# Attention into a SwiGLU feed-forward on one core: a held product, an earlier Sqrt table, a transposed weight row, and half of each swap issued by GpSimd

## Chip, cores, metric

The kernel runs on 1 core of a Trainium2 chip. The metric is the device time in microseconds (us) of one execution, lower is better. Medians of several fast executions are quoted. The span of a profile is about 1.8 us shorter than the time of the same execution. One execution of the kernel before took 559.56 us; it is counted as disturbed, and medians and ratios here leave it out.

TensorE is PE below, VectorE DVE, ScalarE ACT, GpSimd Pool, SyncE SP. PSUM is the memory in which PE leaves its results until DVE or ACT has read them.

## The reference

```python
# q, k, v: (8, 12, 448, 64) float32
scores = q @ k.transpose(0, 1, 3, 2) / sqrt(64)
attn   = maximum(scores, 0) ** 2 / 448
x      = (attn @ v)                    # -> (8 * 448, 768), heads side by side
rms    = sqrt(mean(x * x, -1) + 1e-6)
xn     = x / rms * rms_g
g, val = xn @ w_gate, xn @ w_val       # 768 -> 1536 each
out    = (silu(g) * val) @ w_out       # 1536 -> 768
```

## The kernel before

A block is one of the 8 batch entries (b). While PE runs the gate and value matmuls of block b, the scores and values of block b + 1 are woven in as side tasks; then come output tiles, during which the normalisation of block b + 1 is done. `fb` counts the 12 column blocks of 128 gate and value columns.

Gate and value matmuls are 64 rows deep. Gate uses one half of PE's rows and value the other at the same time, so x is needed in both halves: `xT`, and `xD`, in which the two partition halves have changed places. For blocks 2 to 7 that exchange is done by DMA on the normed x.

```python
def leave(b, js):                       # attention values out of PSUM, on ACT
    ...
    if b > 1:
        square()
    for i, j in enumerate(js):
        nc.scalar.mul(out=xTs[b][:, j, :], in_=psAV[:, i, :], mul=ga_sb[:, j : j + 1])
    if b < 2:
        square()

def swap(b, j0, j1, eng=None):
    for hf in (0, 1):
        (eng or nc.sync).dma_start(
            out=xDs[b][hf * HALF : (hf + 1) * HALF, j0:j1, :],
            in_=xTs[b][(1 - hf) * HALF : (2 - hf) * HALF, j0:j1, :])

def norm_stat(b, ...):                  # sum of squares by PE, then
    nc.scalar.activation(out=half[:], in_=psSS, func=ACT.Sqrt, ...)
    nc.scalar.activation(out=warm_act[:], in_=eps_col[:], func=ACT.Silu)   # loads the Silu table
    nc.vector.reciprocal(out=half[:], in_=half[:])
    ...                                 # spread over partitions, scale x, swap

def blocnpart(b, fb, r0, r1):           # a unit: 2 of 12 rounds in blocks 1 to 7
    if r0 == 0:
        gvs[b, fb] = [ps_m.tile(...) for nm in ("psG", "psV")]   # 4 buffers: two pairs
    rounds(b, fb, gvs[b, fb], r0, r1)
    if r1 < 2 * KT:
        return
    ...
    nc.scalar.activation(out=s[:], in_=psG, func=ACT.Silu)
    nc.vector.tensor_tensor(out=hT[:, fb, o : o + S], in0=s[:], in1=psV, op=ALU.mult)

# weaving, NB = 72 units of gate and value
sides += along(0, (NB - 1) / len(steps), steps[:-3])        # attention of the next block
sides += [(NB - 1, steps[-3]), (NB - 0, steps[-2]), (NB, steps[-1])]
sides += [(NB + 2, norm_stat of b + 1), (NB + 2.1, norm_apply of b + 1)]   # cut to its sense
```

Of the kernel before, what the change touches and what calls it, by code (L numbers as in the profile page):

```python
# [8 lines left out]
FP32 = mybir.dt.float32  # L9
BF16 = mybir.dt.bfloat16  # L10
ALU = mybir.AluOpType
# [23 lines left out]
def kernel(  # L35
# [11 lines left out]
    nc = tc.nc  # L47
# [240 lines left out]
    def leave(b, js):  # L288

        psAV = psAVs.pop((b, js))  # L290
        last = (b, js[0]) == (0, HP - 1)

        def squares_of(i0, i1, o):
            nc.scalar.activation(out=o, in_=psAV[:, i0:i1, :], func=ACT.Square, scale=inv_attn)

        def square():
            if b < 2:
                squares_of(0, len(js), x2s[b][:, js[0] : js[-1] + 1, :])
                return
            t = sums[b]  # L300
            if js[0] == 0:
                squares_of(0, 2, t[:])
                return
            two = npool.tile([P, 2, S], FP32, name="x2f", tag="x2")
            for i in range(2):
                o = two[:, i, :]
                squares_of(i, i + 1, o)
                if js[0] == 2:
                    nc.vector.tensor_tensor(out=t[:, i, :], in0=t[:, i, :], in1=o, op=ALU.add)
                    if i:  # L310
                        nc.vector.tensor_tensor(
                            out=t[:, 0, :], in0=t[:, 0, :], in1=t[:, 1, :], op=ALU.add
                        )
                else:
                    nc.vector.tensor_tensor(out=t[:, 0, :], in0=t[:, 0, :], in1=o, op=ALU.add)

        if last:
            square()
            low, high, every = slice(0, HALF), slice(HALF, P), slice(0, P)
            j = js[0]  # L320
            for dst, to, fr in ((xTs, every, every), (xDs, low, high), (xDs, high, low)):
                nc.vector.tensor_scalar_mul(
                    out=dst[b][to, j, :], in0=psAV[fr, 0, :], scalar1=ga_sb[fr, j : j + 1]
# [5 lines that stand above are left out]
            nc.scalar.mul(out=xTs[b][:, j, :], in_=psAV[:, i, :], mul=ga_sb[:, j : j + 1])  # L329
        if b < 2:  # L330
            square()

    def cross(b, j, psAV):

# [1 line left out]
        for to, fr in ((low, high), (high, low)):  # L336
            nc.scalar.mul(out=xDs[b][to, j, :], in_=psAV[fr, 0, :], mul=ga_sb[fr, j : j + 1])

    def swap(b, j0, j1, eng=None):

        for hf in (0, 1):
            (eng or nc.sync).dma_start(
                out=xDs[b][hf * HALF : (hf + 1) * HALF, j0:j1, :],
                in_=xTs[b][(1 - hf) * HALF : (2 - hf) * HALF, j0:j1, :],
            )
# [166 lines left out]
    def rounds(b, fb, parts, r0, r1, x=None):  # L512

        for r in range(r0, r1):
            kt, own = r % KT, r < KT
            src = (x or (xTs[b], xDs[b]))[0 if own else 1]
            for part in range(2):
                prt = slice(part * HALF, (part + 1) * HALF)
                h = 2 * kt + (part if own else 1 - part)
                nc.tensor.matmul(  # L520
                    out=parts[part][:, :S],
                    lhsT=wgv_sb[prt, h, fb * P : (fb + 1) * P],
                    rhs=src[prt, kt, :],
                    start=(r == 0),
                    stop=(r == 2 * KT - 1),
                )
# [27 lines left out]
    def blocnpart(b, fb, r0, r1):  # L554
        if r0 == 0:
            gvs[b, fb] = [
                ps_m.tile([P, S], FP32, name=nm, tag="mm")[:] for nm in ("psG", "psV")
            ]
        rounds(b, fb, gvs[b, fb], r0, r1)
        if r1 < 2 * KT:  # L560
            return
        psG, psV = gvs.pop((b, fb))
        s = spool.tile([P, S], BF16, name="sil", tag="sil")
        nc.scalar.activation(out=s[:], in_=psG, func=ACT.Silu)  # L564
        hT, o = hidden(b)
        nc.vector.tensor_tensor(out=hT[:, fb, o : o + S], in0=s[:], in1=psV, op=ALU.mult)  # L566

    osts = {}

    def outproj(i, t, o, w):  # L570
# [59 lines left out]
    with fpool as fp:  # L630
        for nm, src, eng in (("k", k, nc.sync), ("q", q, nc.scalar)):
            first[nm] = fp.tile([PC, 2, NCH * D], FP32, name="first_" + nm, tag="first_" + nm)
            eng.dma_start(out=first[nm][:], in_=head_rows(src, 0, 0, 2))
        g_sb = wpool.tile([P, KT], FP32, name="g_sb", tag="rmsg")
        nc.sync.dma_start(out=g_sb[:], in_=moe_rms_g.rearrange("(kt p) -> p kt", p=P))
        load("k", 0, 2, 4)
        load("q", 0, 2, 4)
        ident = const.tile([PC, PC], BF16, name="ident", tag="ident")
        masks.make_identity(nc, ident[:])
        warm_in = const.tile([P, S], BF16, name="warm_in", tag="warm_in")  # L640
        nc.vector.memset(warm_in[:], 0.0)
        ones_bf = const.tile([P, P], BF16, name="ones_bf", tag="ones_bf")
        nc.vector.memset(ones_bf[:], 1.0)
        eps_col = const.tile([P, 1], FP32, name="eps_col", tag="eps_col")
        nc.vector.memset(eps_col[:], eps)
        warm_act = const.tile([P, 1], FP32, name="warm_act", tag="warm_act")
        nc.scalar.activation(out=warm_act[:], in_=eps_col[:], func=ACT.Sqrt)
        nc.vector.tensor_copy(out=ld["k", 0][:, :2, :], in_=first["k"][:])
        nc.scalar.copy(out=ld["q", 0][:, :2, :], in_=first["q"][:])
    ga_sb = wpool.tile([P, KT], FP32, name="ga_sb", tag="rmsga")  # L650
    nc.vector.tensor_scalar_mul(out=ga_sb[:], in0=g_sb[:], scalar1=inv_attn)
    load("k", 0, 4, 6)
    load("q", 0, 4, 6)
    load("v", 0, 0, 6)
    load("k", 0, 6, 12)
    load("q", 0, 6, 12)
    load("v", 0, 6, 12)

    def warm(n):

# [23 lines left out]
    with tc.tile_pool(name="qkT", bufs=2, side="right") as tp, tc.tile_pool(  # L684
        name="early", bufs=EB, side="right"
    ) as ep:
        late["qkT"], late["early"] = tp, ep
        warm(12)
        steps = attention_second(1)

        def early_block(fb):
            return [ps_m.tile([P, S], FP32, name="psE", tag="mm")[:] for _ in range(2)]

        units = attention_first(0)
        tail = len(units) - 4
        for n, fn in enumerate(units[:tail]):
            fn()
            if n % 3 == 2 and n < tail - 1:
                warm(2)


        raw_x = xTs[0], xDs[0]
        psSS = ps_m.tile([P, S], FP32, name="psSS", tag="mm")
        blocks = [early_block(0)]

        def part(fb, *rs):
            for r in rs:
                rounds(0, fb, blocks[fb], r, r + 1, raw_x)

        psAV4 = psAVs[0, (HP - 2,)]  # L710
        squares_last, leave_4, attend_5, leave_5 = units[tail:]
        squares_last()
        part(0, *range(HP - 2))
        pe_transposes(1, 0)
        leave_4()
        attend_5()
        leave_5()
        cross(0, HP - 2, psAV4)
        part(0, KT, HP - 2, KT + 1, KT + 2)
        norm_stat(0, psSS, steps.pop(0))  # L720
        norm_spread(0)
        blocks.append(early_block(1))
        part(1, *range(KT))
        part(0, HP - 1)
        part(1, *range(KT, KT + 3))
        part(0, KT + 4)
        steps.pop(0)()
        part(1, KT + 4)
        norm_apply(0)
        for fb in range(2):  # L730
            part(fb, KT + 3, KT + 5)
            early_out(0, fb, blocks[fb])
            if fb == 0:
                pe_transposes(1, 1)
        for fb in range(2, EB):
            blocks.append(early_block(fb))
            for r0 in range(0, 2 * KT, KT):
                steps.pop(0)()
                rounds(0, fb, blocks[fb], r0, r0 + KT, raw_x)
            early_out(0, fb, blocks[fb])  # L740
        main = gate_value(0, EB, KT // 2)
        sides = along(6.4, 2, [lambda fb=fb: early_scale(0, fb) for fb in range(EB)])
        sides += along(10.4, 2, [lambda fb=fb: early_rest(0, fb) for fb in range(EB)])
        sides += along(0, (len(main) - 1) / len(steps), steps[:-1])
        sides += [(26, lambda: trans_fill(2, 0))]
        alloc_ld(2)
        load("q", 2)
        load("k", 2)
        for s in range(4, FT // 2):
            fetch_o(s)  # L750
        sides += [(26, lambda: load("v", 2))]
        weave(main, sides)
# [55 lines left out]
```

## Time and profile before

| | before |
|---|---|
| median of fast executions | 443.1 to 443.5 us in the different sets of runs |
| span of the profile, first scores, end of PE | 441.23, 6.73, 437.19 us |
| PE from its first output matmul to its end | 363.20 us |

The prediction below shows the main lines. The step that a stall on the scores makes, in PE's timeline (start, length, engine, line, operation, output and inputs, shapes, count):

```profile
162.20 0.35 PE L520 MATMUL psV<-xD,wgv_sb 64*128 64x448 bf16 x1
162.62 0.36 PE L228 MATMUL psS<-qT,kT 64*128 64x448 bf16 x2
```

```profile
91.86 0.35 PE L520 MATMUL psG<-xT,wgv_sb 64*128 64x448 bf16 x1
92.05 0.35 PE L520 MATMUL psV<-xT,wgv_sb 64*128 64x448 bf16 x1
```

### The profile page before, as it was taken

Reading aid. Unit: us, or ns where it says so; the run is one execution under the profiler, and the core shown is the slowest. Engines: PE = TensorE matmul, PEld = TensorE weight load, DVE = VectorE, ACT = ScalarE, POOL = GpSimd, SP = SyncE. Lnnn points to the kernel's source line nnn. Section 1 sums busy time; section 2 is a strip of 40 time slices with the busy share of each in tenths; the row PEclk is TensorE's granted clock in tenths of the full one; section 3 lists DMA queues with packets and bytes.
Section 4 is the critical chain, followed back from the end, with each engine's and each line's share of the span. In section 5 each row is a group of like instructions: output and inputs, shape, how many; then the busy total and the mean of one; then the engine's idle time right before and its main releaser. Section 6 shows DMA issues by size and latency. Waiting matters only on the chain.

```text
span 441.2 us, 10928 instructions
## 1 busy us (share of the span) xinstructions
PE 431.9 (98%) x4718; PEld 248.6 (56%) x4718; DVE 288.8 (65%) x387; ACT 287.6 (65%) x445; POOL 53.7 (12%) x79
## 2 busy tenths in 40 slices
PE   7999999999999999999999999999999999999996
PEld 3345555655566555655566555655557555665664
DVE  4989975777863867766864768577775468742211
ACT  4899886676584775777765776767766677552220
POOL 8343300030001200021000300003000000000000
PEclk9999999999999999999999999999999999999999
DMA  9999999999117991189904997169903900041013
GB/s 135 196 207 198 197 211 186 199 177 182 33 37 157 208 153 33 37 182 169 149 15 96 188 207 95 36 108 224 164 18 78 206 20 1 1 116 57 1 37 109
DMA packets 87632, 53.21 MB, mean 121 GB/s; under 512 B 36768, under 2 KB 83232, under 8 KB 87584
## 3 DMA queue, kind: packets, MB, share of 16 engines
q0 software_dynamic: 44496, 27.50, 43.2%
q1 hardware_dynamic: 42464, 24.44, 28.1%
q8 instruction: 37, 0.61, 0.6%
q10 hardware_dynamic: 624, 0.57, 0.4%
q14 instruction: 11, 0.09, 0.1%
HBM read 47.19 MB, written 11.01 MB: 132 GB/s over the span
## 4 chain that ended last, share of the span: by engine, by line
PE 86%; ACT 7%; DVE 4%; issue 1%; DMA 1%; SPq 0%; ACTq 0%; DVEq 0%
PE psG L520 30%; PE psO L435 23%; PE psV L520 13%; PE psAV L273 9%; PE psS L228 6%; ACT r L217 2%; PE psW L663 2%; DVE r L240 1%; PE psS L187 1%; ACT r L197 1%; ACT sil L564 1%; DVE hT L566 1%; DMA xD<-xT 1%; DVE xT L500 1%; PE psT L143 1%
## 5 line engine op out<-in xcount | busy, mean ns | idle before, releaser
L520 PEld LDWEIGHTS <-wgv_sb 64*128 64x128 bf16 x2304 | 125.2, 94 | 95.6 <-issue 8.3
L520 PE MATMUL psV<-xD,wgv_sb 64*128 64x448 bf16 x558 | 128.4, 349 | 0.4 <-DMA xD<-xT 0.4
L520 PE MATMUL psG<-xD,wgv_sb 64*128 64x448 bf16 x558 | 128.5, 349 | 0.0
L520 PE MATMUL psG<-xT,wgv_sb 64*128 64x448 bf16 x558 | 128.4, 349 | 0.0
L520 PE MATMUL psV<-xT,wgv_sb 64*128 64x448 bf16 x558 | 128.0, 349 | 0.1
L242 ACT ACTIVATE r<-psS 112x896 bf16<-112x896 f32 x108 | 99.1, 918 | 20.5 <-PE psS L228 17.9
L435 PE MATMUL psO<-wo_sb,hT 128*64 128x512 bf16 (+2 forms) x1368 | 111.8, 323 | 0.0
L566 DVE TENSOR_TENSOR hT<-sil,psV 128x448 bf16<-128x448 bf16 x93 | 57.4, 618 | 62.6 <-ACT sil L564 62.6
L246 DVE TENSOR_TENSOR r<-r 112x1792 bf16<-112x1792 bf16 x72 | 78.0, 1088 | 29.2 <-ACT r L242 28.8
L435 PEld LDWEIGHTS <-hT 128*64 128x64 bf16 x1368 | 74.9, 110 | 35.6 <-issue 0.4
L564 ACT ACTIVATE sil<-psG 128x448 bf16<-128x448 f32 x93 | 50.5, 543 | 58.6 <-PE psV L520 35.5
L228 PE MATMUL psS<-qT,kT 64*128 64x448 bf16 (+1 forms) x288 | 56.1, 350 | 0.4
L587 ACT COPY ost<-psO 128x512 f32<-128x512 f32 (+1 forms) x54 | 25.1, 477 | 39.8 <-PE psO L435 39.8
L273 PE MATMUL psAV<-r,vb 112*64 112x448 bf16 x384 | 40.3, 355 | 0.0
L240 DVE TENSOR_SCALAR r<-psS 112x896 bf16<-112x896 f32 x36 | 39.0, 1084 | 1.9 <-PE psS L228 1.9
L175 POOL DMA_DIRECT2D qT<-qT x12 | 6.5, 541 | 263.5 <-PE psS L228 154.1
L273 PEld LDWEIGHTS <-vb 112*64 112x64 bf16 x384 | 20.1, 109 | 18.6 <-issue 6.5
L329 ACT ACTIVATE xT<-psAV,ga_sb 128x448 bf16<-128x448 f32 x47 | 27.8, 647 | 3.9 <-PE psAV L273 3.8
L228 PEld LDWEIGHTS <-kT 64*128 64x128 bf16 (+1 forms) x288 | 19.0, 97 | 16.0 <-issue 4.9
L500 DVE TENSOR_TENSOR xT<-xT,rstd 128x448 bf16<-128x448 bf16 x48 | 26.4, 619 | 2.3 <-ACT rstd L488 2.3
L471 DVE RECIPROCAL rhalf<-rhalf 128x224 f32<-128x224 f32 x8 | 12.4, 1553 | 21.3 <-ACT rhalf L465 21.3
L256 DVE TENSOR_TENSOR r<-r 112x1792 bf16<-112x1792 bf16 x23 | 24.3, 1083 | 0.7 <-ACT r L217 0.7
(68 smaller groups left out, 278.4 us busy)
## 6 DMA issues: line engine op xcount, KB each, us to landing
vb<-in_v_dram POOLq DMA_DIRECT2D x7, 672.0 KB, 18.4
xD<-xT SPq DMA_DIRECT2D x42, 112.0 KB, 2.3
qb<-in_q_dram POOLq DMA_DIRECT2D x6, 672.0 KB, 11.9
kb<-in_k_dram POOLq DMA_DIRECT2D x6, 672.0 KB, 14.5
qT<-qT POOLq DMA_DIRECT2D x24, 168.0 KB, 3.4
out_dram<-ost SPq DMA_DIRECT2D x7, 336.0 KB, 4.7
wgv_sb<-in_moe_w_gate_dram POOLq DMA_DIRECT2D x6, 384.0 KB, 16.9
wgv_sb<-in_moe_w_val_dram POOLq DMA_DIRECT2D x6, 384.0 KB, 16.9
```

Of the source, the lines that this page charges most:

```text
L228: nc.tensor.matmul(out=psS[: end - o, hf, :S], lhsT=flat[prt, o:end], rhs=qT[prt, 1 - hf : 3 - hf, h % HH], start=True, stop=True,)
L240: nc.vector.tensor_relu(out=r[:, cp], in_=src)
L242: nc.scalar.activation(out=r[:, cp], in_=src, func=ACT.Relu)
L246: nc.vector.tensor_tensor(out=r[:], in0=r[:], in1=r[:], op=ALU.mult)
L273: nc.tensor.matmul(out=part[hh * D : (hh + 1) * D, :], lhsT=ld["v", b][:, 2 * j + hh, c * D : (c + 1) * D], rhs=rsq[b, 2 * j + hh, c], sta ...
L329: nc.scalar.mul(out=xTs[b][:, j, :], in_=psAV[:, i, :], mul=ga_sb[:, j : j + 1])
L435: nc.tensor.matmul(out=ps[prt, :w], lhsT=lhsT[:, prt], rhs=rhs, start=start, stop=stop)
L500: nc.vector.tensor_tensor(out=x[:, kt, :], in0=raw_x[:, kt, :], in1=rstds[b][:], op=ALU.mult)
L520: nc.tensor.matmul(out=parts[part][:, :S], lhsT=wgv_sb[prt, h, fb * P : (fb + 1) * P], rhs=src[prt, kt, :], start=(r == 0), stop=(r == 2 * ...
L564: nc.scalar.activation(out=s[:], in_=psG, func=ACT.Silu)
L566: nc.vector.tensor_tensor(out=hT[:, fb, o : o + S], in0=s[:], in1=psV, op=ALU.mult)
L587: (nc.vector.tensor_copy if last else nc.scalar.copy)(out=osts[i, t][:, o : o + w], in_=ps[:, :w])
```

## The change

Four things: DVE's product of a column block is held back until after the next unit's matmuls; the Sqrt table is loaded at the end of a block's attention; the row of norm weights is loaded as 6 rows of 128 and transposed on PE; one of the two DMAs of each swap of the normed x is issued by Pool.

```diff
@@ leave
         if b < 2:
             square()
+        if b and js[-1] == HP - 1:
+            nc.scalar.activation(out=warm_act[:], in_=eps_col[:], func=ACT.Sqrt)
@@
-    def swap(b, j0, j1, eng=None):
-        for hf in (0, 1):
-            (eng or nc.sync).dma_start(
+    def swap(b, j0, j1):
+        for hf, eng in enumerate((nc.sync, nc.gpsimd if b > 1 else nc.sync)):
+            eng.dma_start(
@@ blocnpart
         rounds(b, fb, gvs[b, fb], r0, r1)
+        while held:
+            held.pop()()
         if r1 < 2 * KT:
             return
 ...
-        nc.vector.tensor_tensor(out=hT[:, fb, o : o + S], in0=s[:], in1=psV, op=ALU.mult)
+        def product():
+            nc.vector.tensor_tensor(out=hT[:, fb, o : o + S], in0=s[:], in1=psV, op=ALU.mult)
+        if b > -1 and fb < FT - 1:
+            held.append(product)
+        else:
+            product()
@@ start
-        g_sb = wpool.tile([P, KT], ...)
-        nc.sync.dma_start(out=g_sb[:], in_=moe_rms_g.rearrange("(kt p) -> p kt", p=P))
+        g_rows = wpool.tile([KT, P], ...)
+        nc.sync.dma_start(out=g_rows[:], in_=moe_rms_g.rearrange("(kt p) -> kt p", p=P))
 ...
-    nc.vector.tensor_scalar_mul(out=ga_sb[:], in0=g_sb[:], scalar1=inv_attn)
+    ident_g = const.tile([KT, KT], ...);  nc.vector.tensor_copy(out=ident_g[:], in_=ident[:KT, :KT])
+    def columns_of_g():                 # after the first transposes of q and k
+        psg = ps_m.tile([P, KT], FP32, name="psg", tag="mm")
+        nc.tensor.transpose(out=psg[:], in_=g_rows[:], identity=ident_g[:])
+        nc.vector.tensor_scalar_mul(out=ga_sb[:], in0=psg[:], scalar1=inv_attn)
```

More of the change, by code (lines that the diff above doesn't have):

```diff
@@ L565, in blocnpart @@
         hT, o = hidden(b)
-        nc.vector.tensor_tensor(out=hT[:, fb, o : o + S], in0=s[:], in1=psV, op=ALU.mult)
+        def product():
[4 more added lines that the diff above has]
+            product()
+    held = []
     osts = {}
@@ L633 @@
             eng.dma_start(out=first[nm][:], in_=head_rows(src, 0, 0, 2))
-        g_sb = wpool.tile([P, KT], FP32, name="g_sb", tag="rmsg")
-        nc.sync.dma_start(out=g_sb[:], in_=moe_rms_g.rearrange("(kt p) -> p kt", p=P))
+        g_rows = wpool.tile([KT, P], FP32, name="g_rows", tag="rmsg")
+        nc.sync.dma_start(out=g_rows[:], in_=moe_rms_g.rearrange("(kt p) -> kt p", p=P))
         load("k", 0, 2, 4)
@@ L650 @@
     ga_sb = wpool.tile([P, KT], FP32, name="ga_sb", tag="rmsga")
-    nc.vector.tensor_scalar_mul(out=ga_sb[:], in0=g_sb[:], scalar1=inv_attn)
+    ident_g = const.tile([KT, KT], FP32, name="ident_g", tag="ident_g")
+    nc.vector.tensor_copy(out=ident_g[:], in_=ident[:KT, :KT])
     load("k", 0, 4, 6)
@@ L697 @@
             fn()
+            if n == 0:
+                columns_of_g()
             if n % 3 == 2 and n < tail - 1:
```

## The prediction

> **What bounds the kernel now.** I read the page first: busy time per engine, then the chain of work that ended last.
>
> ```profile
> PE 431.9 (98%) x4718; PEld 248.6 (56%) x4718; DVE 288.8 (65%) x387; ACT 287.6 (65%) x445; POOL 53.7 (12%) x79
> ...
> PE 86%; ACT 7%; DVE 4%; issue 1%; DMA 1%; SPq 0%; ACTq 0%; DVEq 0%
> ```
>
> The first row says that TensorE (PE) shows work in 431.9 of 441.2 us; VectorE (DVE), ScalarE (ACT) and GpSimd (Pool) have room. The second says that the chain back from the last instruction lies on PE for 86% of the span. Nothing in the diff takes away a large matmul, so the change can only gain where PE stands still or steps late.
>
> Busy time hides much of that, because matmuls overlap and their ends are modelled. So I used the timeline of PE and measured from start to start. Two 64-row matmuls run side by side, and a pair starts every 0.19 us. A longer step is a stall, and the excess over 0.19 us is what it costs. Going through all steps after the first 60 us, the ones with an excess of 0.1 us or more are few. One, of 0.14 us at 68.2 us in block 0, has no wait on the change's path. The others are of three kinds.
>
> First kind, once in each of blocks 1 to 6 (at 109.2, 162.2, 212.1, 265.1, 314.2 and 367.2 us), here in block 2 by the chain of waits:
>
> ```profile
> 160.38 0.55 ACT sil L564
> 160.94 0.62 DVE hT L566
> 161.57 1.01 DVE r L240
> 162.62 0.36 PE psS L228 x2
> ```
>
> The columns are start, length and work. PE's score matmul at 162.62 waits for a PSUM buffer that the relu (L240) on DVE empties. In the timeline this relu's input is ready at about 160.5 (its scores start at 160.11 and take 0.35), but DVE executes in order and the product before it (L566) waits for the Silu (L564). PE's step from 162.20 to 162.62 is 0.424 us, so the excess is 0.234 us.
>
> Second kind, the halves of the normed x that swap places by DMA (xD<-xT), in block 3, by the same chain:
>
> ```profile
> 188.57 0.58 SPq L342
> 189.25 0.55 SPq L342
> 189.85 3.40 DMA xD<-xT
> 193.29 0.35 PE psV L520
> ```
>
> and by PE's timeline:
>
> ```profile
> 191.78 0.35 PE L520 MATMUL psG<-xD,wgv_sb 64*128 64x448 bf16 x1
> 192.33 0.35 PE L520 MATMUL psV<-xD,wgv_sb 64*128 64x448 bf16 x1 [0.20 <-DMA xD<-xT]
> ...
> 193.29 0.35 PE L520 MATMUL psV<-xD,wgv_sb 64*128 64x448 bf16 x1 [0.22 <-DMA xD<-xT]
> ```
>
> SP issues six of these DMAs, one about every 0.6 us, while DVE produces a pair's input every 1.1 us. The steps here are 0.550 and 0.569 us, an excess of 0.36 and 0.38. Block 7 has a small one at 396.6 us (0.299, excess 0.11). Waits longer by the page's measure look smaller (0.20 and 0.22) because an earlier matmul is still drawn as running; I trust the starts.
>
> Third kind: at 398.26 us, 0.313 us, excess 0.12. PSUM for the third column block waits for the product of the first, 0.54 us of Silu and 0.62 of product after the last matmul. No other DVE work is near, so the change can't move it.
>
> **What the Trainium skill says.** "DMA: Bandwidth & Descriptors", section "Issuing engines are not separate DMA queues": DMAs issued by different engines run on the same 16 DMA engines, and issuing from several saves only issue time. The trace agrees as far as it can: the swap is bound by six issues of about 0.6 us behind one another, and that is all I count as saved. The same page, "SWDGE vs HWDGE vs iDMA", describes descriptors that Pool has to compute in software, so the Pool half could land later. Here the first of Pool's two fills of qT (168 KB, larger than a swap half of 112 KB as listed) lands 2.5 to 2.6 us after issue where little else moves, against 2.1 to 2.3 us for undisturbed SP halves: 0.3 us worse, not more.
>
> "ScalarE: Activation LUTs", "What ACT_TABLE_LOAD costs": 1283 ns for a load, plus a drain of about 1.4 us. The trace has 1283 ns exactly; the drain is not seen in it, since ScalarE goes on 0.1 us after a load.
>
> "TensorE: Matmul & The Clock Gate", "Back-to-back issue gap": N/2.4 + 2.5 ns warm, 189 ns for 448 columns, the 0.19 us per pair above. So PE has no slower steps to recover inside the stream.
>
> **The change, part by part.**
>
> Holding back the product (hT) until after the next unit's matmuls: no work added or removed, 85 of the 93 products of this line (all but the last of each of eight blocks) move later in DVE's order. In the first kind of stall the relu can start at about 160.6 rather than 161.5 and end at 161.7, before PE would ask for the buffer at 162.39. The product then runs from about 161.7 to 162.4 instead of to 161.56. Its PSUM pair is next needed a whole column block later, about 163.1 in this block, so it is still in time. Gain: 6 x 0.234 = 1.40 us, all on PE's path.
>
> One swap DMA of each pair by Pool, in blocks 2 to 7. Eighteen issues move. SP then issues three, each as its input is ready, and the last pair goes out at the same time on both queues. In block 3 the last issue would be at about 188.6 rather than at 189.85. Pool's queue is in order and carries the qT fills, which wait for long (up to 30.3 us), but in program order the swaps come before the fill that waits; the earlier fill had gone out at 164.34 in this block. So they aren't caught behind it.
>
> The Sqrt table load moves to right after the attention of a block: 7 loads stay 7, and 7 dummy activations of 0.2 us are added. Block 3 before:
>
> ```profile
> 179.36 0.59 ACT L587 COPY ost<-psO 128x512 f32<-128x512 f32 x1 [0.16 <-PE psO L435]
> 180.67 0.37 ACT L587 COPY ost<-psO 128x256 f32<-128x256 f32 x1 [0.72 <-PE psO L435]
> 181.06 1.28 ACT L465 ACT_TABLE_LOAD   x1
> 182.35 0.45 ACT L465 ACTIVATE rhalf<-psSS,eps_col 128x224 f32<-128x224 f32 x1
> ```
>
> After it, the load would take 179.2 to 180.5 and the dummy to 180.7; the two copies then end at about 181.3 and 181.65, and Sqrt starts there instead of at 182.35. The copies are pushed, so the gain is 0.7 us and not 1.28. Everything that follows on DVE (reciprocal, scaling by rstd, swap) comes 0.7 us sooner. By itself it only takes away slack, as PE is in output matmuls all this time. But with Pool's help the last swap of block 3 is issued about 187.9 and lands by about 190.5, or 192.3 if an instruction fetch of 16 KB is in its way again as in this block (one transfer took 1.2 us on one DMA engine at 189.8, another 1.8 us in block 4 at 237.6). PE wants the last pair at about 192.3 once nothing before has stalled. Gain of the two together: 0.36 + 0.38 + 0.11 = 0.85 us, of which I expect nearly all.
>
> The gain g read as 6 rows and transposed on PE: it takes away a DMA of 768 packets of 4 bytes that landed 4.0 us after issue, and an early DVE wait of 0.37 us. PE's warm-up matmuls last until about 5.55 us and the second cast, on ACT, ends at 5.64 us, so the first transposes can't come more than 0.1 us sooner. Added: one small matmul and one small DVE copy, in a stretch where PE waits 0.64 us and DVE 0.65 us anyway. Net gain 0.1 us.
>
> Sum: 1.40 + 0.85 + 0.10 = 2.35 us. 443.52 - 2.35 = 441.2 us, 0.5% less.
>
> **The rivals.** (a) The held product becomes the new wait. It frees PSUM later by up to one DVE instruction of 1.09 us, and in block 0 DVE and ACT are at seven to nine tenths busy and PE already has steps 0.2 to 0.5 us late around 51 to 57 us. Against it: in blocks 1 to 6 a side task lies between a product and its new place for only about four of twelve column blocks, and a PSUM pair has some 2.3 us to come free where 1.2 are used. If it failed there each time, six blocks by 0.2 us plus 1 us in block 0 would give back the 2.35 and the time would stay at 443.5. (b) Pool's half lands late: software descriptors, an engine that wakes slower. If each Pool half came 1.5 us later than SP's, blocks 3, 5 and 7, which have three output tiles and not four ahead of them, would still stall by some 0.3 to 0.8 us: 442.2. (c) The gain moves elsewhere: PE arrives earlier at a wait that was hidden by the one removed, for instance another scores buffer one visit later. Then half of the 1.40 is lost: 441.9. (d) More than I count: the missing g packets speed up the first loads, and all of the start shifts by 0.5 us: 440.8. The warm-up matmuls speak against it.
>
> **Range and chances.** PE's unmoved stream fixes the time; all stalls I can name sum to some 3 us after 60 us, so faster by 2% (8.9 us) can't come from here. Losing 2% would take a new stall of over 1 us in every block. Same kernel, different runs: 443.1 and 443.52 (the third, 559.56, I take for a disturbed run). With (a) to (c) above and this scatter: 439.9 to 442.9.
>
> **What would show it.** L240's relu starting before the product, and no step of 0.42 us ahead of the scores in blocks 1 to 6; Pool issuing 18 swaps, the third pair's two issues within 0.2 us of each other; no wait of psV on xD<-xT; the L465 loads gone, seven loads at the leave line, Sqrt 0.7 us sooner after its sum; first scores at 6.6 to 6.7 us. PE busy stays within 1 us of 431.9 and the span falls by 2 to 2.5. Wrong would be: new steps of PE waiting for the product, swap landings by Pool of over 3.5 us, or a span within 1 us of the old.

## More of the kernel before

Gate and value normally start within 0.02 us of each other. Here, at the start of column block 2 in block 1 (PE's timeline at 91.86 us), value starts 0.18 us after gate, since its PSUM buffer waits for the product of column block 0, which DVE ends at 91.99:

```profile
91.37 0.62 DVE L566 TENSOR_TENSOR hT<-sil,psV 128x448 bf16<-128x448 bf16 x1
```

From there on the value half runs behind. A list of start-to-start steps of all matmuls together doesn't show this as a gap. It has to be paid where the next operation needs both halves.

## The result

441.83 us median (441.65 to 442.09, 4 runs), against 443.52 us for the kernel before (443.10 to 443.87, its 3 fast runs; 443.69 where the disturbed run is counted). The ratio is 0.9963, with a 95% interval of 0.9943 to 0.9982. Ratios here are the mean time of one kernel's fast runs over that of the other's of the same rounds, so not quite the ratio of the medians quoted.

The span in the profile fell less, from 441.23 to 440.18 us. That is made of three parts: first scores 0.47 us later (7.20), PE from there to its end 1.91 us shorter (430.45 to 428.54), and the time from PE's end to the span's end 0.39 us longer (4.44). The part from the first output matmul to the end of PE went from 363.20 to 361.28 us, 1.92 less.

The page after, the rows that answer to the two at the top of the prediction:

```profile
PE 431.7 (98%) x4719; PEld 253.0 (57%) x4719; DVE 287.6 (65%) x388; ACT 287.7 (65%) x452; POOL 63.2 (14%) x97
...
PE 92%; ACT 6%; issue 1%; DVE 0%; DVEq 0%
```

Busy times are the same; DVE (4% before) and the swap DMAs are gone from the chain.

Stall on the scores, DVE's timeline of block 2 after:

```profile
160.74 1.08 DVE L240 TENSOR_SCALAR r<-psS 112x896 bf16<-112x896 f32 x1
161.74 0.61 DVE L572 TENSOR_TENSOR hT<-sil,psV 128x448 bf16<-128x448 bf16 x1
```

The relu now starts at 160.74 and ends before the scores (162.60 in this profile, one normal step after the matmul before). The product comes after it. But in each of blocks 1 to 6 there is a new wait, shown here in block 1, PE's timeline:

```profile
115.62 0.35 PE L522 MATMUL psV<-xD,wgv_sb 64*128 64x448 bf16 x1
115.80 0.35 PE L522 MATMUL psG<-xT,wgv_sb 64*128 64x448 bf16 x1
115.93 0.35 PE L522 MATMUL psV<-xT,wgv_sb 64*128 64x448 bf16 x1
```

and DVE's timeline that leads up to it, the kernel after first and the kernel before second:

```profile
113.07 1.08 DVE L240 TENSOR_SCALAR r<-psS 112x896 bf16<-112x896 f32 x1
114.25 1.09 DVE L246 TENSOR_TENSOR r<-r 112x1792 bf16<-112x1792 bf16 x1
115.26 0.61 DVE L572 TENSOR_TENSOR hT<-sil,psV 128x448 bf16<-128x448 bf16 x1
```

```profile
112.94 1.08 DVE L240 TENSOR_SCALAR r<-psS 112x896 bf16<-112x896 f32 x1
113.94 0.61 DVE L566 TENSOR_TENSOR hT<-sil,psV 128x448 bf16<-128x448 bf16 x1
114.47 2.13 DVE L246 TENSOR_TENSOR r<-r 112x1792 bf16<-112x1792 bf16 x2
```

The held product now sits behind a square of 1.09 us (L246) and ends at 115.87; value's matmul starts at 115.93, 0.12 us after its usual place, and this half of PE stays behind by 0.12 us until the values of the attention, which need both halves.

Sqrt in block 3, ACT's timeline, answering to the four lines of the prediction:

```profile
179.30 1.28 ACT L333 ACT_TABLE_LOAD   x1
180.59 0.20 ACT L333 ACTIVATE warm_act<-eps_col 128x1 f32<-128x1 f32 x1
180.70 0.84 ACT L599 COPY ost<-psO 128x512 f32<-128x512 f32 x2
181.43 0.46 ACT L467 ACTIVATE rhalf<-psSS,eps_col 128x224 f32<-128x224 f32 x1
```

Sqrt starts at 181.43, 0.92 us sooner. The swaps of block 3 follow, SP's queue and Pool's:

```profile
185.50 2.60 SPq L344 DMA_DIRECT2D xD<-xT  x3
```

```profile
186.01 0.52 POOL L344 DMA_DIRECT2D xD<-xT  x1 [21.22 <-DVE xT L502]
...
187.90 0.52 POOL L344 DMA_DIRECT2D xD<-xT  x1 [0.55 <-DVE xT L502]
```

The last one goes out at 187.90 rather than at 189.85. PE waits for no swap any more; its waits in this profile are four entries, all in the first 58 us.

### The profile page after: what moved, and what is told of

It is laid out like the page before. It is cut to its first block, busy times and chain, and to the rows that moved or that the text cites. A ratio compares the mean times of both kernels' runs of the same rounds, so it can differ in the third digit from the quotient of the medians.

```text
span 440.2 us, 10948 instructions
## 1 busy us (share of the span) xinstructions
PE 431.7 (98%) x4719; PEld 253.0 (57%) x4719; DVE 287.6 (65%) x388; ACT 287.7 (65%) x452; POOL 63.2 (14%) x97
## 4 chain that ended last, share of the span: by engine, by line
PE 92%; ACT 6%; issue 1%; DVE 0%; DVEq 0%
PE psG L522 28%; PE psO L437 25%; PE psV L522 18%; PE psAV L273 9%; PE psS L228 6%; ACT r L217 2%; PE psW L682 2%; PE psS L187 1%; ACT r L197 1%; PE psT L143 1%; PE psS L207 1%; ACT qkT L151 1%; ACT gv L534 1%; PE psSS L463 1%; PE psE L522 0%
## 5 line engine op out<-in xcount | busy, mean ns | idle before, releaser
L522 PEld LDWEIGHTS <-wgv_sb 64*128 64x128 bf16 x2304 | 129.8, 94 | 93.4 <-issue 8.7
L246 DVE TENSOR_TENSOR r<-r 112x1792 bf16<-112x1792 bf16 x72 | 78.2, 1087 | 35.0 <-ACT r L242 34.4
L228 PE MATMUL psS<-qT,kT 64*128 64x448 bf16 (+1 forms) x288 | 58.5, 349 | 0.0
L344 POOL DMA_DIRECT2D xD<-xT x18 | 9.4, 524 | 147.4 <-DVE xT L502 104.1
```

The lines of the kernel that those rows point to most:

```text
L228: nc.tensor.matmul(out=psS[: end - o, hf, :S], lhsT=flat[prt, o:end], rhs=qT[prt, 1 - hf : 3 - hf, h % HH], start=True, stop=True,)
L246: nc.vector.tensor_tensor(out=r[:], in0=r[:], in1=r[:], op=ALU.mult)
L522: nc.tensor.matmul(out=parts[part][:, :S], lhsT=wgv_sb[prt, h, fb * P : (fb + 1) * P], rhs=src[prt, kt, :], start=(r == 0), stop=(r == 2 * ...
```

## Experiments

All runs gave the correct result. "To end" is PE from its first scores to its end, "steady" PE from its first output matmul to its end, "tail" from there to the end of the span; these are of the one profile of each run. "Clock up" is when the granted clock rises to full, from the trace's clock record.

| run | median us | ratio to before, 95% | clock up | first scores | to end | steady | tail |
|---|---|---|---|---|---|---|---|
| before | 443.1 to 443.5 | | 5.19 | 6.73 | 430.45 | 363.20 | 4.05 |
| after | 441.83 | 0.9963 (0.9943 to 0.9982) | 6.79 | 7.20 | 428.54 | 361.28 | 4.44 |
| only_hold | 442.33 | 0.9980 (0.9968 to 0.9992) | 6.54 | 7.18 | 429.04 | 361.78 | 4.26 |
| only_pool | 443.44 | 1.0009 (0.9995 to 1.0023) | 7.04 | 7.20 | 429.96 | 362.70 | 5.28 |
| only_sqrt | 442.72 | 0.9991 (0.9979 to 1.0003) | 4.16 | 6.48 | 429.92 | 362.40 | 4.39 |
| only_g | 443.16 | 1.0003 (0.9991 to 1.0014) | 6.40 | 7.18 | 430.57 | 363.31 | 3.99 |
| again | 441.76 | 0.9967 (0.9954 to 0.9979) | 6.41 | 7.17 | 428.52 | 361.29 | 4.28 |
| hold_six | 441.21 | 0.9955 (0.9942 to 0.9969) | 5.38 | 6.83 | 427.94 | 360.71 | 4.35 |
| six_visit | 440.88 | 0.9946 (0.9934 to 0.9959) | 4.78 | 6.53 | 428.17 | 360.69 | 4.40 |
| hold_two | 441.18 | 0.9947 (0.9935 to 0.9960) | 4.95 | 6.61 | 428.36 | 360.67 | 4.33 |
| no_pool | 441.60 | 0.9960 (0.9948 to 0.9972) | 5.25 | 6.76 | 428.55 | 361.30 | 4.25 |
| no_sqrt | 442.15 | 0.9971 (0.9959 to 0.9982) | 5.44 | 6.85 | 428.69 | 361.44 | 4.68 |
| two_six | 441.10 | 0.9943 (0.9930 to 0.9956) | 4.57 | 6.42 | 428.56 | 360.56 | 4.31 |
| two_six_visit | 440.04 | 0.9921 (0.9908 to 0.9934) | 6.79 | 7.20 | 426.81 | 359.55 | 4.40 |

**The four parts alone.** Each edit is that part of the diff above, put on the kernel before.

*only_hold*

> Only the held product is added to the kernel before. Theory 1 (from the two traces: the six stalls of 0.234 us ahead of the scores go, but in each of the six blocks the psV stream gets a new wait of about 0.12 us for the held product, paid at the next full-array matmul): 0.12 us less per block, 0.7 us in all, ratio 0.998; steps of the psV stream of 0.31 us near the end of each of blocks 1 to 6, PE 0.12 us further ahead after each block. Rival (the prediction as written: no new wait): 1.4 us less. Rival (the hold does nothing on balance): within 0.2 us. The stalls on xD<-xT at about 192 us stay under all.

Steady time 1.42 us less, but 0.42 of that is the swap stalls, which happened to be smaller in this profile (by 0.37 us in block 3 and 0.05 in block 7). In blocks 2, 4, 5 and 6, where no swap stalls, the period from one block's output matmuls to the next's fell by 0.15 to 0.17 us (53.01 to 52.86 in block 2), in block 1 by 0.21. All the psV steps of 0.31 us are there. So the hold is worth 1.0 us of the 1.40 predicted, not 0.7 either. The ratio of 0.998 that was expected came by luck: in this profile the hold's 1.0 us and the 0.42 of the swaps stand against a start 0.45 us later and a tail 0.21 us longer.

*only_pool*

> Only the second DMA of each swap goes to Pool. Theory (the wait for xD in block 3 was the six issues behind one another on SP): the last pair is issued at about 188.6 on both queues, the 0.36 us stall goes and of the 0.38 us one 0.0 to 0.35 stays if the instruction fetch lies in the way: 0.5 to 0.85 us less. Rival (Pool lands too late, or the time came from the earlier Sqrt): within 0.2 us. Rival (noise of where instruction fetches fall explains block 3): no stall or another one in this profile of before-like blocks, unrelated to who issues.

Steady time 0.50 us less: block 3 keeps a stall of 0.38 us (its last pair landed 4.0 us after issue, at 193.0 and 193.3), block 7's is gone. But only_hold, without Pool, has 0.40 us left in block 3, so this one profile does not show that Pool shortened that stall. The execution times show no gain. This profile has the longest tail of all, 5.28 us, with two store issues of 1.34 and 1.50 us on SP and ACT that took 0.64 and 0.60 before. Why is open; no other kernel with the Pool swap has it (4.28 to 4.68).

*only_sqrt*

> Only the Sqrt table load moves. Theory: Sqrt 0.7 us sooner after the sum, swaps issued 0.7 us sooner by SP; the stalls of block 3 (0.36 and 0.38) shrink by 0.7 together at most, the one of block 7 (0.11) goes: 0.4 to 0.8 us less. Rival (it only takes away slack): within 0.2 us.

Steady time 0.80 us less. In block 3 one stall is left, in PE's timeline:

```profile
192.29 0.35 PE L522 MATMUL psG<-xD,wgv_sb 64*128 64x448 bf16 x1
192.63 0.35 PE L522 MATMUL psV<-xD,wgv_sb 64*128 64x448 bf16 x1
```

0.34 instead of 0.19. Its last swap landed at 192.59, 3.8 us after issue. That is less than the three profiles with neither part have in block 3 (0.40 to 0.90 us). That the earlier Sqrt does more than Pool is what these single profiles suggest; they don't show it. By the execution times only_sqrt gains 0.4 us, with an interval that includes zero.

*only_g*

> Only g is read as 6 rows and transposed on PE. The kernel after had its first scores at 7.20 us, not 6.73, with PE's clock raised at 6.8 us after the first instruction rather than 5.2. Theory[...]: first scores at 6.6 to 7.3 us depending on when the clock is raised in this profile; time within 0.3 us of before. Rival (the g part itself delays the start, by its transposed copy or the identity): first scores at 7.2 us or later even with the clock raised at about 5.2, 0.5 us more. Rival (the prediction): 0.1 us less.

Nothing gained, nothing lost: the ratio is 1.0003, and PE takes 67.26 us from the first scores to the first output matmul with and without it. The start depends on the clock. The kernel here has g transposed and a late clock; only_sqrt has g as before and an early clock. PE's timelines:

```profile
5.75 0.58 PE L143 MATMUL psT<-ident,kb 112*64 112x112 bf16 x8
...
7.18 0.37 PE L187 MATMUL psS<-qkT 64*128 64x448 bf16 x2 [0.40 <-DVE qkT L149]
```

```profile
4.99 0.39 PE L143 MATMUL psT<-ident,kb 112*64 112x112 bf16 x8
...
6.48 0.55 PE L187 MATMUL psS<-qkT 64*128 64x448 bf16 x4 [0.49 <-DVE qkT L149]
```

The same eight transposes take 0.58 and 0.39 us. only_hold and only_pool, which have g as before, also start at 7.18 and 7.20 with a late clock, so that start isn't the g part's. The converse is in the later runs: kernels with g transposed start at 6.42 to 6.85 where the clock rose before 5.5 us.

**The changed kernel, varied.**

*again*: no edit.

> The changed kernel once more, unaltered. Theory (start and end move by chance, the stream of PE between them doesn't): the time from the first scores to the end of PE is 428.5 us again within 0.2, the first scores lie at 6.5 to 7.2 us with the moment at which the clock is raised, the end takes 4.0 to 5.3 us; ratio to before 0.996 to 0.997. Rival (the start of 7.20 us belongs to this kernel): 7.2 us again although the clock is raised at 5.2 us or earlier.

It repeats within 0.02 us in both PE columns. The clock was late again, so this run alone doesn't settle the rival on the start; hold_six and the others with g transposed do.

*hold_six*:

```diff
-        if b > -1 and fb < FT - 1:
+        if b > 0 and fb == 6:
             held.append(product)
```

> The changed kernel, with only the product of column block 6 of blocks 1 to 6 held back, the one in front of the relu that PE waits for. Theory 1 (the products of other column blocks, held behind a square of 1.09 us, make psV wait 0.12 us at the start of the next but two column blocks): the stalls of 0.234 us stay away and the steps of 0.31 us of psV go too; PE's time from first scores to end 0.3 to 0.7 us less than the changed kernel's 428.5. Rival (the wait is block 6's own): steps of 0.31 us as before, no gain. Rival (all products have to be held): stalls of 0.23 us come back.

The edit also holds block 7's product, where no scores are woven in, and none in block 0, which steady time leaves out. The psV steps of 0.31 us are gone, and so are the 0.23 us stalls. Steady time 0.57 us below the changed kernel's; a block's period is 52.76 instead of 52.86. Only the product ahead of the awaited relu needs to be held. Others being held is the new wait.

*six_visit*: in addition

```diff
             sides += along(0, (NB - 1) / len(steps), steps[:-3])
+            sides[5] = (12, sides[5][1])
```

> As the one before, and the sixth side task (a pair of score matmuls) is put ahead of the first matmul of column block 2 instead of one unit after it. Theory (psV there waits 0.17 us for the product of column block 0, the lag stays with one half of PE's rows and is paid at the next full-height matmuls): 0.19 us of other work fills the wait, the steps of 0.36 us ahead of block 2 shrink to 0.19, up to 0.15 us less in each of blocks 1 to 6, 0.9 us in all below hold_six. Rival (the lag costs nothing, being beside another wait): no change. Rival (the scores come too early for their buffer): a new step of 0.2 us or more at that place.

No change in steady time. The lag at column block 2 is gone, but the scores some 5 us later wait 0.18 us on both halves instead of on one. In hold_six that wait stood beside the lag. My first theory falls here: the lag was not the only thing in its place.

*hold_two*:

```diff
-        while held:
-            held.pop()()
+        while len(held) > (r0 == 0):
+            held.pop(0)()
```

> The changed kernel with each product held for two units instead of one: the suspected cost doubled. Theory 1 (PSUM comes free later by what is held in front): the psV steps of 0.31 us grow or become more in number, PE's time 0.5 us or more above the changed kernel's. Rival (the new wait has nothing to do with how long a product is held): same as the changed kernel within 0.2 us.

(The units of column blocks 0 and 1 are interleaved, so column block 0's product is still held for one unit.) The opposite of the theory came: steady time 0.61 us less and no psV step of 0.31 us. So it isn't how long a product is held. DVE's timeline in block 1:

```profile
111.04 1.09 DVE L246 TENSOR_TENSOR r<-r 112x1792 bf16<-112x1792 bf16 x1 [0.60 <-ACT r L242]
112.05 0.62 DVE L572 TENSOR_TENSOR hT<-sil,psV 128x448 bf16<-128x448 bf16 x1
112.58 1.09 DVE L240 TENSOR_SCALAR r<-psS 112x896 bf16<-112x896 f32 x1
```

In the changed kernel the product there came first, at 111.53 after 1.03 us of idle time waiting for the Silu, and the square behind it at 112.07. Here the square fills that idle time. All that follows comes sooner: the product that value waits for ends at 115.39, ahead of its matmul at 115.76, rather than at 115.87 when PE was ready at 115.81. What counts is the order of DVE's queue, and which wait stands at its head.

*no_pool* (both DMAs of a swap by SP: `(nc.sync, nc.sync)`) and *no_sqrt* (the two lines in `leave` taken out):

> The changed kernel with both DMAs of every swap issued by SP again; the earlier Sqrt, the held product and g stay. Theory (the two work together; alone the earlier Sqrt left a stall of 0.16 us in block 3): a stall of 0.1 to 0.3 us on xD<-xT in block 3 and none in block 7, PE's time from first scores to end 428.6 to 428.9 us, within 0.3 us of the changed kernel. Rival (Pool's half is what saves the time): 0.7 us or more above 428.5. Rival (Pool's share is worth nothing once Sqrt is early): 428.5 within 0.05.

> The changed kernel with the Sqrt load back in its old place; Pool, held product and g stay. Theory: swaps issued 0.7 us later, a stall of 0.2 to 0.5 us in block 3, small or none in block 7, PE's time 428.7 to 429.1 us. Rival (Pool alone suffices): 428.5.

no_pool: no stall at all and the same steady time as the changed kernel (361.30 against 361.28 and 361.29). The six issues of SP in block 3:

```profile
185.07 4.03 SPq L344 DMA_DIRECT2D xD<-xT  x6
```

They end at 189.10, and the last swap lands at 191.74, in time. no_sqrt: one stall of 0.12 us in block 3, 0.16 us in all. With the other parts there, Pool's half is worth nothing that could be measured and the earlier Sqrt 0.15 us, in one profile each; the intervals of the ratios of both take in the changed kernel's 0.9963.

*two_six* (as hold_six, `fb in (2, 6)`) and *two_six_visit* (that with the moved side task):

> As hold_six, with the product of column block 2 held as well: the control for the next run. Theory (the scores of the first half of a block wait for a relu behind that product, but this lies beside the lag of psV, which is paid anyway at the next full-height matmul): the steps of 0.37 us ahead of the scores at about 97, 150, 199 us go, PE's time 427.9 us within 0.2. Rival (these waits do cost): 0.5 to 1.0 us less.

> As the one before, and the pair of score matmuls put ahead of column block 2, as in six_visit, where the wait only moved to the scores half a block later (steps of 0.37 us on both halves). Theory (two waits lie side by side, each 0.18 us; only removing both gains): neither the psV steps of 0.36 nor the score steps of 0.37 are left in blocks 1 to 6, 0.15 to 0.18 us less in each, PE's time 427.0 us within 0.3 (up to 0.3 more if the start is early and block 0 waits for its loads), ratio to before 0.992 to 0.994. Rival (a third wait takes their place): 427.9 again.

two_six: the score waits of 0.37 us are gone and steady time is 0.15 us below hold_six, so they were indeed beside the lag. Its time from first scores to end shows no gain, because its early start is given back in block 0, as PE's list of waits (line waited for: total, times, longest) says:

```profile
PE psT L143 <- DMA qb<-in_q_dram: 0.8, 1, 0.8
```

two_six_visit: both are gone, and blocks 1 to 6 have no step left that is out of place by more than the change between matmul kinds. A block's period is 52.57 us, against 53.01 before and 52.86 after the change. It is the best of all: 440.04 us, ratio 0.9921 to before. That is 1.73 us of steady time below the changed kernel.

## Why the prediction was right, and which of its terms was off

The time fell inside the range (441.83 against 441.2, range 439.9 to 442.9), and the mechanism was right in the main: the stalls on the scores and on the swaps went. Some of its own signs of being wrong came all the same: new steps of PE waiting for the product, and halves issued by Pool that took over 3.5 us to land (4.09 in block 3, 4.36 in block 4). The span fell by 1.05 us and not by 2 to 2.5, since the start came 0.47 us later and the tail took 0.39 us more; both scatter from profile to profile. The sum was 2.35 us; PE's stream shows 1.92, and the two sets of times 1.5 to 1.6 by their ratios, with an interval from 0.8 to 2.5 us for the first. The 1.92 has some luck in it: with the swap stalls of only_hold, 0.42 us smaller, it would have been 1.5 (an estimate).

- **The held product, "6 x 0.234 = 1.40 us, all on PE's path": mis-sized, it measured 1.0 us.** The stalls went. The words "it is still in time" failed: rival (a), the held product as the new wait, came with 0.12 us where it names 0.2, at a later column block of each of blocks 1 to 6, and not in block 0. The estimate checked the slack of the column block whose product is held at the stall (it is in time, by hold_six), but not each of the others, where a square is ahead in the queue. Rival (c) is not what took the rest: no score step out of place is left in blocks 1 to 6. Also unseen was the lag of one half of PE. Block 2 has the balance: its period was 0.44 us above that of two_six_visit before (0.18 of score wait with the lag beside it, 0.234 of stall), and 0.29 after (0.17 of lag now paid by itself, 0.12 of the new wait).
- **The swaps, 0.85 us: right in size for this profile, off in what made them late and in who does it.** Block 3's period fell by 0.93 us, of which 0.15 is the hold, and block 7's by 0.13: 0.91 us. The prediction took six issues of SP behind one another for the bound. no_pool has the same six issues, only sooner, and no stall. What was late was the landing: the last three halves in block 3 took 3.3 to 3.7 us instead of 2.3, with an instruction fetch under way (see the last section), which the prediction had named only as a risk. At 2.3 us the last of them, issued at 189.85, would have landed at 192.15, before the 192.3 at which PE wanted it (an estimate). Issuing sooner leaves room for such a delay: in the seven profiles with both parts there is no stall in block 3. The earlier Sqrt with the rest of the change does it without Pool (no_pool), Pool without Sqrt does most of it (no_sqrt). The stall itself isn't fixed: by block 3's period it was 0.77 us in the kernel before, 0.40 in only_hold and 0.90 in only_g, whose swaps are the same three pairs from SP, each with a fetch under way. So the share of each part is not shown.
- **Sqrt 0.7 us sooner: it was 0.92.** The two copies take 0.84 us together, not the 0.95 reckoned, and Sqrt starts 0.11 us before their end.
- **g, 0.10 us: nothing.** In its place the clock moved the first scores between 6.42 and 7.20 us in 14 profiles. The start is partly given back when early, as PE then waits for its loads in block 0. Rival (d) did not come.
- **Rival (b), Pool late:** no. In blocks 2 to 7 Pool's 18 halves landed after 2.45 us in the median and SP's after 2.29, less apart than the 0.3 us estimated. The late ones in block 4 were SP's as much as Pool's (4.28 and 4.36 us), with a fetch under way.
- **The skill's issue gap.** In the Trainium skill's "TensorE: Matmul & The Clock Gate", the section "Back-to-back issue gap" gives the formula that the prediction used for an isolated matmul, and says that at large N it over-counts in a stream. Here each half of PE steps by 0.19 us in the stream, as the formula has it.
- What I can't account for is why the execution times of only_pool show no gain where its steady part gained 0.5 us, and what makes the tail 4.0 to 5.3 us long.

## What to carry to other kernels

When two engines' halves or row groups run side by side, measure each stream's steps by itself: a lag of one of them is invisible in the common list and swallows what is gained elsewhere until a full-height operation makes both meet. A wait that is removed uncovers the one beside it, so look for pairs and take away both; here, on top of hold_six, either alone gave 0.0 to 0.15 us and both together 1.2. Moving an instruction back in an in-order queue should be done at the one place where something is awaited behind it, and by asking which wait will then stand at the head of the queue, not everywhere.

## What the Trainium skill lacked or had wrong

- "ScalarE: Activation LUTs", section "What ACT_TABLE_LOAD costs": the load of 1283 ns agrees to the nanosecond; the drain of some 1380 ns after it does not show here. In block 3 the next activation starts 0.01 us after the load ends (180.58, 180.59), as after all 32 loads of the profiles before and after (the prediction's 0.1 us is a misreading), and an early load costs 1.28 plus a dummy of 0.20 us.
- "Runtime: NRT & Kernel Launch", section "Instruction fetch mechanics": calls the cost of crossing a 16 KiB boundary mostly hidden. For PE itself no run here speaks against it, but other DMAs are late beside such a fetch. The 37 packets of 16 KB in the kernel before took 0.88 to 1.79 us each, and in every profile one starts 0.65 to 1.4 us after block 3 begins (at 189.80 us before). In all 14 profiles each swap half of blocks 2 to 7 that took over 3.3 us to land (up to 4.4, instead of 2.3) had such a packet under way. No run moved a fetch, so that it is the cause is inferred. That these 37 are PE's program is inferred from their number too (37 times the page's 256 instructions is 9472, PE has 9436 matmuls and weight loads).
- No page states it: two row halves that run at the same time can drift apart by 0.12 to 0.18 us, here for 5 to 8 us, when only one waits, and no gap shows until both are needed. The half that did not wait was never more than one step of 0.19 us ahead: where value waited longer (192.33 in block 3 before), gate's next matmul came late with it.
